# Gated mix of attention and a 2-D Fourier filter: 83 entries of a stored instruction order moved

## The chip, the cores and the metric

The kernel runs on one core of a Trainium2 chip. The core has five engines with an instruction stream each: TensorE (PE in the profile; its weight loads are PEld), VectorE (DVE), ScalarE (ACT), GpSimd (POOL) and SyncE (SP, which here only issues DMAs). ACT and POOL issue DMAs too. The metric is the device time of one execution in microseconds (us): before, the median of three runs is 454.48 us (454.02 to 456.01).

## The reference, cut to what matters

```
g = sigmoid((x * gate_w).sum(-1, keepdims=True))        # x: 2048 tokens x 640
a = attention(x @ wqkv) @ wo                            # 32 heads of 20, 8 keys: t, t-2, ..., t-14
b = irfft2(rfft2(x, axes=(-2, -1)) * (w_r + 1j * w_i))  # over tokens and features
return g * a + (1 - g) * b
```

All is float32.

## The kernel before, in words

The 2048 tokens lie on 128 partitions as 16 columns j. Everything stays on one core, and everything is written first as a recording: each engine call of the program becomes an entry of a list (`Plan.record`), 3656 in all. Then `Plan.order` reads the constant `ORDER`, a packed row of 3656 numbers. Number k says at which place of the list of what is left the k-th entry is taken out, so that this row alone fixes in which order every engine gets its instructions. `Plan.issue` emits them in that order. Each engine runs its own instructions in the order given; only semaphores, which the tile framework derives from the data and from the reuse of buffers, tie one engine to another. All instructions therefore carry one line in the profile, L385, the line that replays a recorded call, and are told apart by the names of their tiles.

The stages, by the recorded program:

- `warm`: six matmuls on zeros before the first data are there. `load_first`, `qkv_first`, `qkv`: the projection x @ wqkv, each float32 operand split in two parts of fewer bits, three products per pair. `fold`: the inputs x are loaded again (`fx0` to `fx7`, on SP's queue) and added and subtracted in mirrored pairs by DVE and POOL, for the transform along features; the raw weights `raw` come over the same queue, and ACT and POOL make the two parts `w` of them. `cols`: the transform along tokens on TensorE, copied by ACT to `zg`.
- `attend`: the sliding attention, on DVE (products `pr`, sums `L`, `s`, `o`), POOL (`pv`, scaling) and ACT (exponentials). It runs from the first third to the end beside all other stages.
- `freq(g)`, the filter groups g = 1, 2, 3, 0, 4, ..., 15, staged so that four are under way. ACT copies a slice of `zg` to `zc`; TensorE makes `v` and `u`; ACT copies `v` to `vs`; DVE forms the sum and difference `ab`; TensorE makes `x` and `z`; ACT copies `x` to `P` and, multiplied by a sign, `x` and `z` to `X`; two DMAs, issued by ACT, bring the two halves of `X` to the other half of the partitions of `P`. When both have landed, POOL multiplies `P` by the filter `wp` and adds; DVE multiplies `z` by the filter, subtracts `P`, and makes `s` of the sum and difference; TensorE transforms back in five matmuls in two pieces, `g_0` (three) and `g_3` (two), and ACT copies each piece back to `zg`. `P` and `wp` have two buffers each. The PSUM banks are one for each of `v`, `u`, `x`, two for `z`, and one for `g`, so that `g_3` of a group waits for the copy of `g_0`, and `g_0` of the next group for the copy of `g_3`.
- `load_wo`, `project_even`: the output weights `wo` are cast by ACT to their upper part and POOL subtracts to get the lower; attention rows `ot` are transposed on TensorE (`oTp`), cast by ACT to `oT` (upper part), DVE subtracts for the lower; then 15 matmuls each for `woa` and `wob`, scaled by ACT to `ya`. These lie between the filter groups.
- `spatial` (`oa`, `ob`, `ha`, `hb`) and `project_odd`: the inverse transform along features and the other half of the output projection. They close the kernel.

What a number behind a name means in the rows of an order: `P9_727` is the tile P of group 9; `oT4` belongs to token column 4.

Of the kernel before, what the change touches and what calls it, by code (L numbers as in the profile page):

```python
# [201 lines left out]


ORDER = """
T>t<81poj4|NsC0{{R31`zHT%QmDPnN2o4pqG()raQ#vzl-5Q;_f%qBd^O|&eY9QYNBMzhpDJzgbo`p?)i=NlGkg4pi)v=r_Ivh`ry`@DAn{UL<7u-|?Aw}>x~K3VSb)B{-t!WAHm))%
unAhPz4I@-2Iqv#r6L>*Xc$=jvaqQRa3b^|A+Y|WKIEEj)A@6T&9m8<23aOsCR{jD@6j{sYkO?P$b#=n<341!34nZ(X=zG8UQ{qx&71|KC<t@Gco9Z^27=SGu?TP9^_xx9CA@>m7>f!s
OYWHey&#0g11et`Jku?peeD*XENp#NW~XmY)%EME)U$cKF-Z+vV9cFqn%}p&i5#r2B6?^!L$|KiDwS5{;Iff+MQp5qs5Z*^S1D?*FMGw`(SU6f9U%OiawS(-I{rACR8a0gV^g7l@8l@~
HzRC&nZHU65UcUOIO2OqBvnhaDtej1FV1NTEP#T^)e}_RXD9Ad$LgUK7O`DNW0Ah#+vteaZ7c}l&kv=txQ?dKiO=nUU)rA`8g}=!rq`Zp$UL}3=^*VzL;nRihjg*C<t}3f%b%>5e(rGT
7-9+d=Oy~il~(PiH+y=E9&IDY*4qH(EzJ@9f5sB<6JsOb8wgocoqVcb9ZqwjK27E(DzK)a!$n^bod6w(!li>{GgdFyCb^9iu%ubjZcf$uR^!DIu<=bFg$M~+%M&!@`CRf64gryh?xA;L
=GNZz41miwBNJRJ$_PkjO#GJm*8$7Wigq;fww-$@)=FqJsud(o66Kud*z2J1AyupW9GFt;JT~7#Xc;~qw*2h&<S<LPTrE0Tvv;yIwrz$dgfpLZm!26FS+ez!;5Pt$ymK)}uVU7^YB(23  # L210
abfI)oPtr{Wh!}VC7Toq2amz>-c68x1BbhR&{(ROO)>dDpl%@SkBwsg>XhKMqNltvxU8}VnLD-Mepq&s&h0shElS}Kp$)vXuTq>iX>Cb3wH*5XM0KNCE>o-pp4<I`M~`Jd4t7#L9b*fF
wuGdJat(T)z>igeMB8%*RWQ2i06@>6iiY1>U5b|2v0EKBb^l^DfU!qWovI!Z)z_$mF)>18`>*Fx>5l*lLUh^2W>YVO>m}WBw^64&l77+nuC39&CM|*NV;F&Kj^Ppbsxdr{UH3QiDdtoE
>9^Z^(}BqP7lK<BR!aE$l*Cn@sqW=Rrb62!JRq@AUQ**c44zhaQ@t%%#OaD#xOULbqH7cNBRcpC$<;6ezVESAzEV6VDilz>dquhr&==?Ggiw{Z9m#%FDOMWi=7=f>RgP8@SK-o)kAgWc
@(~x_1gJz+dYwk6|3WH!Q+8xdEtnm+stHe=6)34-WpZL}4ugdfpv6H=3ArGy{O4l+-$ydmOvz{guh;2O#|DKW?>s2?n#?x#3TACjF=U2+g*kOcry4r$vD>c_(rzX7C1gGLLs}3NQZAtv
ogzd_!bABa9T?T3Gs=$zHA+BgpwKT1x1UyIm=uw*eDoI2ukgn(P$?v&8zZ+rqRW+=JglNr!n`th?ETZV$#&=i{iwkUtIaB@Q}*NHX-6O2z+m$sMuH>Wz2^1n{cpGSFz=vH&jcSfoL*PT
l(e3=1WK!@5fXav8#wz>T7U{iN<IAmx<(?^C_>kP7N|hYIekD3RBcpw0FDjy^s|gj!DtD#|Fe=A_=*%<#m8R@<Wb!hJG2mfgFIL-rE+7}MD)%GRQf34Eqq=3$hY_fP({XdfJ|XhJkGh*
;rddl98_KAxC_7a!PrDj$BdC~u?on-Sr!%7x<Xb-%|fGLYD;nbsQhFH`ZV2!AwjD5oZh`s>-nQReDf92g(!@sE)9XSby_X}JZC};N5m{&=tv2y?|{U!Xo}XY=9BhrsO)i~RVAUM^Zq|O
U<q^R{Fq9K0g(^bS~-#Ar7l~w9U*|gOjae1XA9=)^;WNww^WC#4NH>zmLFJ{KLbF2L~M-}VOHY45$&O!e^N2K+6x=vhq?zH#-*SPa7QY%j-TtZnWJ-SP%t-ngyr>5zN0GFY5WDlJ6xVY
J{?Q+DnkgL|4!{Sm<~W1m{#H-i#v+$kXc^Td=7heyIz#Z=u004G<&&-oRvQN>@ufMHq^=_nd~Lslju>7E|fryCi!(_@>ZcR_(2!-ffb6vQBf?!jJJpypg#Pl(ICI9d_*^JoFXsY5wOvi
nr1gFTCsh?1Z_h$3nMfvh8Bme$@%=-h{q?O6}Gk2hmQOegP}ygA~^2Iy=xmWVhfbR01Yc(!EMjd<%9@Vb+3e~4Tp1v+AlQ*{#c5SAYU<n*kAABp<2#cQRW!xhkP$v4+Q_B@o1RR^qZ=!  # L220
KeYQb+1wyz!xaZ;$|p~0Rkw(@l$#UaI{9@wGRt=OVop%vdH&C)f#pnq8#sp}eaD-%4T)cljwr&kWt(1u-yr$^T9|Th^!}&q#YLBhX4!=WaHOIid?(#4<cxl{;tI|VZp<8Df0tkOj5Jg<
zrLM3bspM%T&FVXAT;ePvu{w0-b6_nx;Ueyvynjx&1|1+Tr@Ma=vsZ;Z%(dMHq!G`SSXA%hUbZ0h8CW*EQ16manzQK<G&iL$@&h?N+WhK;95=}$gl<@C*;vSR+Gf_uMhDwcnrx&(<w#E
4@wDP2Sfe^s<4LS9>wv^@!P~EXoURBZ3aW7O{<DH;@bA%XV!^Nl&1lOHC+tpbjZ+jlWz(<xS8p*U7aet(m%YtU&)nda#i2(JfPWkJVFa(3Ltu6dk!#zpbcN{))aMKqsS^Al8l>OF@O~e
x(u+`_%sPsRi0Dl>z$t3^_s&-5k^L24nD#imbvd3lI5somyD;SGYh5p&x~Eea*h2|SPh0<Eb)zkO*`v;lUxAdI~a{fLZN`^G~L~t=1sbS`R;PB!Rn>VoOf64#iStA<yF-d%C;StyT|aY
?D(Tvdj)-E5H7x(%n1xC9d_foxjYSU#`BetY+t-WLnF^a<<=FUKyU@t&wUZ+iyz%aL&8WAup}SL^6`w!wyvn?Wk95WtV9^<2QqBYqe*mJR6-|}h$TGSv<76T!0?!B3R*cOCQAQQsOxdd
m3p$Nr6FlsqZm6&X5wW3>VG@o8cE)9LE34q+962yQajx~L(yyIq<`x{dWPvVOR`<6m}Oj6rZ{<H#`=rZh;|nIj|%8ORTVkOwbj3lhBGbTy@{(rh)-RVDCFQCvIW<2(5~_J)mPX>q56=+
Lhb>Ury!q;u}317-G@VQbSrO2)@wK#*2ey?$}g#2?U)pHv2s)pO?NC$NEZW}_=Pt^aCWSUnecEhx+Ibb?goExm{@-C0R=icvA>d;Lu2H0!_EaXeEKyk9iDqL+QBxor42ZIwFnnqAn6U3
_*)I?j(1Tb0Wru}z21ORZ9XANGt|a9GXRlDTv}|*ARx}4_pIOCIo}-%!+7EO46gQUoEI60HjiILM*_ON0>z=h9(a6jQ;n(if?QQ-d^(IxQa#o>X6Jj%Q~CVQ#tLzt$>!Z+m~oDjH=b%d
EKH_NEnnRB9(XVoDJ*@Zl675mh^pl-iALQ<c#u_7Xo3rfzTZrwxLLtlJ3eToG_xzP!s~I?WSCvyaR;y760%i;da_`9s~x8jv}!Cc#!nD;$8oY;%>}(Xu+}@7MrUZ2xihJzmNgd4?UuqQ
lj=2;{2MzSWldas;&S-TwvkI_^2-P(=+cY8NZ&KM#is{cx5Azh%rCCt_psh>;~#?CtG3B{ge&v5h$2|y{1|MIAK}+Ozghda1$mEgjpr7gMG`_IAOyi2domcj>9vTFM{B)wg*vp8$43or  # L230
Z@f{5Aex(=<zM8D2QRnY(Y^KUX#@f4ZMpYmdi0Miez?%sJ5zGB^D45Fhf?kY{c@1$1BZ*>*+bO7a5u<wOeml`7Zq-=5UqRs_6{m%aRem&IUXR;KBV&N!gweQb9B4c1dkV?z||S$8Y3m`
GISu@RzcTi>)y3qbD1XFKrjX8vHIl7reyxUS`UQ^$iw2TW_U_EB}KkdFu=o|xj{SS9^$%*xDiw}`^K^#mLU;ock7`j`Qj(AEx_NJ_6u4orvtlP9ztAo9qI(|9tWj!A}E0dnKUdKnFwf7
zGmMtKJ1JmDDk~OP7f@*?4vAi$S~Y7QPj-j!`A{ShO;R91xRW^h3#^2+-prcKnN-wL2y2hR88R2htAU;VrO5f#&*@5Bx#>?5C4ph2%gxeNLs<$8e4ZgeQr~$iv#P~$&<JH_MQ%5B)~mR
{qzhlVEVEvM0r60xftwa->^J+OYgZKQ8Ieli{hlUl(tt=31MC3VNY@y-W>Mj&!KTpf7+g&#28y108c2U0qHc4VnD^$I;|}w$0CN*1p_Gc8rT2bkG2*
"""


# [729 lines left out]
```

## Time and profile before

| | before |
|---|---|
| median of three runs | 454.48 us (454.02 to 456.01) |
| profiled execution | 455.9 us, of which the span is 453.8 us |
| TensorE busy | 440.5 us, 97% of the span |
| VectorE busy | 410.4 us, 90% |
| GpSimd busy | 364.4 us, 80% |
| ScalarE busy | 212.4 us, 47% |
| DMA moved | 110.75 MB, 244 GB/s on the mean |

Busy time is the time in which an engine's instructions ran; matmuls overlap, so a busy TensorE is one without a gap and not one at its peak. A row of the timeline gives the start, the length, the engine, and the operation as output tile <- input tiles (buffer numbers left out), with the count of instructions that it joins; a bracket at its end says how long the engine stood idle before it and which operation ended that. One float32 matmul of the program can leave two records. ACTq and SPq are DMA issues of these engines.

### The profile page before, as it was taken

To read this page: it belongs to the slowest core of one execution; us is meant where nothing else is said; L and a number is where in the kernel's file an instruction comes from. 1 tells how busy PE (TensorE), PEld (TensorE's weight loads), DVE (VectorE), ACT (ScalarE), POOL (GpSimd) and SP (SyncE) were. 2 spreads that over 40 slices of the span, in tenths; PEclk is the share of its full clock that TensorE was granted. 3 is DMA by queue.
4 is the path that set the end of the run, shared out by engine and by line. 5 is a ranking of instruction groups with operands and counts; after the bars stand their busy time and mean duration, and the time that the engine had idled before them with its cause. 6 is when DMAs were issued, how large, how long until landed. Compare 5 with 4: busy or idle time off the path is not lost. (4 is left out here: it accounts for less than half of the span.)

```text
span 453.8 us, 7246 instructions
## 1 busy us (share of the span) xinstructions
PE 440.5 (97%) x2440; PEld 390.1 (86%) x2440; DVE 410.4 (90%) x519; ACT 212.4 (47%) x561; POOL 364.4 (80%) x316
## 2 busy tenths in 40 slices
PE   8999999999999999999998999999989999999996
PEld 6888888888888888899886789989877899999996
DVE  4999999799999999999989999989899997899484
ACT  4724254444236454255457665666554554342110
POOL 1158895599999999997987998976999988879720
PEclk9999999999999999999999999999999999999999
DMA  8998999688868989679969888979884231364832
GB/s 317 389 370 285 380 300 379 244 252 284 230 192 259 364 243 315 171 243 315 311 207 290 258 269 262 287 222 315 264 241 105 82 97 59 127 193 137 282 133 87
DMA packets 73956, 110.75 MB, mean 244 GB/s; under 512 B 21296, under 2 KB 50992, under 8 KB 73920
## 3 DMA queue, kind: packets, MB, share of 16 engines
q1 hardware_dynamic: 40192, 69.32, 46.8%
q10 hardware_dynamic: 32816, 36.97, 26.3%
q0 software_dynamic: 912, 4.00, 2.2%
q8 instruction: 19, 0.31, 0.3%
q14 instruction: 17, 0.14, 0.1%
HBM read 72.51 MB, written 32.84 MB: 232 GB/s over the span
## 5 line engine op out<-in xcount | busy, mean ns | idle before, releaser
L385 PE MATMUL qkv<-w,xo 128*128 128x480 f32 (+1 forms) x480 | 110.9, 386 | 0.3 <-ACT zg L385 0.3
L385 PE MATMUL qkv<-w,xe 128*128 128x480 f32 (+1 forms) x474 | 104.3, 381 | 0.0
L385 PEld LDWEIGHTS qkv<-w,xo 128*128 128x128 f32 x480 | 89.8, 189 | 14.3 <-ACT zg L385 0.7
L385 PEld LDWEIGHTS qkv<-w,xe 128*128 128x128 f32 x474 | 89.2, 188 | 14.8 <-ACT xe L385 0.6
L385 ACT COPY ev<-qkv 128x480 f32<-128x480 f32 x64 | 34.8, 556 | 39.7 <-PE qkv L385 31.8
L385 PE MATMUL woa<-wo,oT 128*128 128x320 f32 x240 | 47.2, 318 | 0.5 <-ACT oT L385 0.3
L385 PE MATMUL wob<-wo,oT 128*128 128x320 f32 x240 | 46.9, 315 | 0.2 <-ACT ya L385 0.2
L385 POOL TENSOR_TENSOR P<-P,wp 128x963 f32<-128x963 f32 (+1 forms) x16 | 35.3, 2209 | 6.8 <-DMA P<-X 4.7
L385 PEld LDWEIGHTS woa<-wo,oT 128*128 128x128 f32 x240 | 37.7, 188 | 1.4 <-ACT oT L385 0.6
L385 PEld LDWEIGHTS wob<-wo,oT 128*128 128x128 f32 x240 | 37.8, 188 | 0.6 <-ACT ya L385 0.4
L385 POOL TENSOR_TENSOR fx<-fx 128x160 f32<-128x160 f32 (+1 forms) x16 | 12.8, 817 | 24.0 <-DMA fc<-in_t_fc 16.9
L385 POOL TENSOR_TENSOR w<-raw,w 128x480 fp32r<-128x480 f32 (+1 forms) x20 | 24.8, 1263 | 5.1 <-ACT w L385 5.0
L385 ACT CAST oT<-oTp 128x384 fp32r<-128x384 f32 (+1 forms) x32 | 13.4, 428 | 31.4 <-PE oTp L385 14.6
L385 PEld LDWEIGHTS g<-mm,s 128*128 128x128 f32 x150 | 21.1, 190 | 8.0 <-ACT zg L385 5.6
L385 PE MATMUL g<-mm,s 128*128 128x128 f32 x150 | 23.9, 281 | 3.6 <-ACT zg L385 3.4
L385 DVE TENSOR_TENSOR oT<-oTp,oT 128x384 fp32r<-128x384 f32 (+1 forms) x32 | 15.3, 487 | 10.5 <-ACT oT L385 10.4
L385 PE MATMUL oa<-gt,zg 128*128 128x161 f32 (+1 forms) x96 | 24.0, 344 | 0.0
L385 PE MATMUL ob<-gt,zg 128*128 128x161 f32 (+1 forms) x96 | 22.1, 344 | 0.0
L385 PE MATMUL v<-bt,zc 128*128 128x240 f32 (+2 forms) x96 | 21.1, 325 | 0.4 <-ACT vs L385 0.3
L385 ACT CAST w<-raw 128x480 fp32r<-128x480 f32 (+1 forms) x30 | 17.3, 594 | 8.1 <-PE qkv L385 3.6
L385 PE MATMUL u<-bt,zc 128*128 128x240 f32 (+2 forms) x96 | 20.1, 322 | 0.7 <-DVE ab L385 0.7
L385 DVE TENSOR_TENSOR fx<-fx 128x642 f32<-128x642 f32 (+2 forms) x24 | 19.2, 800 | 0.7
(304 smaller groups left out, 1106.3 us busy)
## 6 DMA issues: line engine op xcount, KB each, us to landing
qkvd<-ev ACTq DMA_DIRECT2D x32, 480.0 KB, 5.2
wp<-in_ws SPq DMA_DIRECT2D x16, 642.0 KB, 5.1
raw<-in_wqkv SPq DMA_DIRECT2D x25, 240.0 KB, 6.9
fx<-in_x SPq DMA_DIRECT2D x8, 641.0 KB, 8.2
ot<-od SPq DMA_DIRECT2D x16, 320.0 KB, 4.0
P<-X ACTq DMA_DIRECT2D x30, 160.5 KB, 4.4
fd<-fx POOLq DMA_DIRECT2D x6, 640.0 KB, 7.0
f<-fd SPq DMA_DIRECT2D x6, 640.0 KB, 6.5
```

The source lines that it names most:

```text
L385: p.dve.memset(w, 0.0)
```

## The change

Only the constant `ORDER` differs. Each engine gets the same instructions as before; 83 of the 3656 entries stand some places earlier or later. Of the text of the constant two lines stand for all, since its characters tell a reader nothing:

```
 ORDER = """
-T>t<81poj4|NsC0{{R31`zHT%QmDPnN2o4pqG()raQ#vzl-5Q;_f%qBd^O|&eY9QYNBMzhpDJzgbo`p?)i=NlGkg4pi)v=r_Ivh`ry`@DAn{UL<7u-|?Aw}>x~K3VSb)B{-t!WAHm))%
...
```

What it does to the engines' own orders is seen at three places below; a minus is a row of before, a plus a row of after, and a row with neither is in both. The other moves are these. At the start the sixth warm-up matmul stands with the five others and no longer between the first projection matmuls. On SP's queue the loads of `fx4` and `fx5` stand behind four of the five loads `raw2_0`, `raw2_2`, `raw2_1`, `raw2_3`, where they stood ahead of all five. Some casts, folds and attention steps change places with a neighbour in the projection stages. In the filter groups a half of `ab2` on VectorE and the reduction `s7b` go ahead of one attention reduction of `L6a`; `pr5a` goes ahead of `ab7`; on TensorE `x13` goes between the matmuls of `g10_0` and ahead of a transposition; on ACT the second `P` DMA of groups 2, 12, 14 and 15 is parted from the first by copies, as in the first place below. Late in the kernel some matmuls of `woa` and `wob` change places.

ACT, filter group 9, beside the transposition for token column 4:

```order
 L385 ACTIVATE X9_730<-z9_729,sign_325 128x321
 L385 ACTIVATE X9_730<-x9_728,sign_325 128x321
-L385 DMA P9_727<-X9_730 64x642 x2
+L385 DMA P9_727<-X9_730 64x642
 L385 COPY zg_211<-g6_3_712 128x32x8
 L385 CAST oT4_831<-oTp0_832 128x384
 L385 COPY vs11_748<-v11_747 128x321
 L385 COPY P9_727<-x9_728 128x321
+L385 DMA P9_727<-X9_730 64x642
 L385 COPY zg_211<-g7_0_724 128x48x8
```

The second of the two DMAs that exchange the halves of group 9 stood right behind the first and now stands behind four ACT instructions: the copy of `g6_3` to `zg`, the cast of `oT4`, and the copies `vs11` and `P9`.

POOL, between the filter multiplications of groups 2 and 3 (`pv7b` is an attention product, `wo6` the lower part of an output weight):

```order
 L385 TENSOR_TENSOR P2_618<-P2_618 128x321
-L385 TENSOR_TENSOR wo6_334<-wor4_339,wo5_333 128x320
+L385 TENSOR_TENSOR pv7b0_495<-vt7b_485,L7b_487 128x8x80
 L385 TENSOR_TENSOR L6a_503<-L6a_503,m6a_508 128x256
-L385 TENSOR_TENSOR pv7b0_495<-vt7b_485,L7b_487 128x8x80 x2
+L385 TENSOR_TENSOR pv7b0_495<-vt7b_485,L7b_487 128x8x80
 L385 TENSOR_TENSOR wo6_334<-wor4_339,wo5_333 128x320
 L385 TENSOR_TENSOR P3_631<-P3_631,wp3_622 128x963
```

Of the two subtractions for output weights that stood ahead of the multiplication of `P3`, one is gone from there; it stands behind the addition of `P4`, two filter groups later.

TensorE, filter group 15 and the projection of token column 8:

```order
 L385 MATMUL v15_800<-bt_326,zc15_799 128x161
 L385 MATMUL u15_802<-bt_326,zc15_799 128x240
+L385 MATMUL g11_0_778<-mm10_731,s11_766 128x128 x3
+L385 MATMUL woa8_849<-wo0_328,oT8_845 128x320
 L385 MATMUL u15_802<-bt_326,zc15_799 128x161
-L385 MATMUL g11_0_778<-mm10_731,s11_766 128x128 x3
-L385 MATMUL woa8_849<-wo0_328,oT8_845 128x320 x3
+L385 MATMUL woa8_849<-wo0_328,oT8_845 128x320 x2
 L385 MATMUL woa8_849<-wo1_329,oT8_845 128x320
```

The three matmuls of `g11_0` and one of `woa8` now stand ahead of one `u15` matmul that stood ahead of them.

## Rows read from the trace of the kernel before

**Rows 1.** Stretches: us, busy us of each engine (instructions), granted clock, DMA share, GB/s.

```profile
10.00:100.00 90.00, 90.00 (x414) 77.67 (x413) 81.97 (x94) 39.53 (x96) 61.05 (x64) 1.00 0.92 324
230.00:350.00 120.00, 112.62 (x680) 98.61 (x679) 112.17 (x168) 74.46 (x211) 104.71 (x83) 1.00 0.83 255
350.00:400.00 50.00, 50.00 (x316) 45.97 (x315) 43.94 (x56) 25.17 (x67) 44.90 (x37) 1.00 0.34 98
```

**Rows 2.** TensorE's waits: us in total, times, longest us.

```profile
PE g L385 <- ACT zg L385: 3.4, 7, 0.9
```

**Rows 3.** Timeline of ACT at group 9: start, us, operation, idle before.

```profile
294.93 1.12 ACTq L385 DMA_DIRECT2D P<-X  x2
296.09 0.37 ACT L385 COPY zg<-g 128x256 f32<-128x256 f32 x1 [1.23 <-PE u L385]
296.36 0.48 ACT L385 CAST oT<-oTp 128x384 fp32r<-128x384 f32 x1
297.04 0.46 ACT L385 COPY P<-x 128x321 f32<-128x321 f32 x1
```

**Rows 4.** Timeline of TensorE at that place (`g` is `g7_0`).

```profile
296.51 0.94 PE L385 MATMUL g<-mm,s 128*128 128x128 f32 x6 [0.59 <-ACT zg L385]
```

**Rows 5.** Timeline of VectorE there (the lower part of `oT4`).

```profile
296.87 0.56 DVE L385 TENSOR_TENSOR oT<-oTp,oT 128x384 fp32r<-128x384 f32 x1 [1.04 <-ACT oT L385]
```

**Rows 6.** Timeline of POOL there (the multiplication of `P9`).

```profile
302.13 2.27 POOL L385 TENSOR_TENSOR P<-P,wp 128x963 f32<-128x963 f32 x1
```

**Rows 7.** Timeline of ACT at group 1.

```profile
237.22 0.47 ACTq L385 DMA_DIRECT2D P<-X  x1
237.48 0.44 ACT L385 COPY P<-x 128x321 f32<-128x321 f32 x1
```

**Rows 8.** Timeline of POOL ahead of the multiplication of `P3`.

```profile
256.92 0.88 POOL L385 TENSOR_TENSOR wo<-wor,wo 128x320 fp32r<-128x320 f32 x1
257.75 2.23 POOL L385 TENSOR_TENSOR P<-P,wp 128x963 f32<-128x963 f32 x1
```

**Rows 9.** The tile P from 250 to 262 us: durations in ns, first and last start.

```profile
L385 ACTq DMA_DIRECT2D P<-X x2: 507/545/583, 250.2 to 250.8; - x2
...
DMA to landing us min/median/max: 4.5/5.4/6.4
```

**Rows 10.** Timeline of VectorE at groups 2, 3 and 0.

```profile
241.35 0.48 DVE L385 TENSOR_TENSOR ab<-u,vs 128x321 f32<-128x321 f32 x1
...
244.37 0.89 DVE L385 TENSOR_TENSOR ab<-u,vs 128x321 f32<-128x321 f32 x2
...
260.02 0.50 DVE L385 TENSOR_TENSOR z<-z,P 128x321 f32<-128x321 f32 x1 [0.69 <-POOL P L385]
```

**Rows 11.** Timeline of TensorE at groups 2, 11 and 13.

```profile
241.99 0.78 PE L385 MATMUL z<-ab,mm 128*128 128x321 f32 x2 [1.01 <-ACT X L385]
...
323.47 0.84 PE L385 MATMUL u<-bt,zc 128*128 128x240 f32 x4
324.51 0.94 PE L385 MATMUL g<-mm,s 128*128 128x128 f32 x6 [0.20 <-ACT zg L385]
...
336.32 0.94 PE L385 MATMUL g<-mm,s 128*128 128x128 f32 x6 [0.93 <-ACT zg L385]
```

**Rows 12.** Timeline of POOL: the multiplications of `P11` and `P14`.

```profile
314.62 2.27 POOL L385 TENSOR_TENSOR P<-P,wp 128x963 f32<-128x963 f32 x1 [2.50 <-DMA P<-X]
...
335.57 2.24 POOL L385 TENSOR_TENSOR P<-P,wp 128x963 f32<-128x963 f32 x1 [0.67 <-DVE oT L385]
```

**Rows 13.** The tile P from 312 to 325 us, its DMA issues.

```profile
L385 ACTq DMA_DIRECT2D P<-X x4: 468/538/1414, 316.6 to 323.2; - x4
```

**Rows 14.** Timeline of SP in the fold stage.

```profile
21.71 6.39 SPq L385 DMA_DIRECT2D raw<-in_wqkv  x5
```

**Rows 15.** The tile fx from 14 to 46 us: issue to landing of its DMAs.

```profile
DMA to landing us min/median/max: 5.0/8.2/11.8
```

**Rows 16.** Timeline of VectorE: the first fold step of `fx4`.

```profile
36.89 1.11 DVE L385 TENSOR_TENSOR fe<-fx 128x642 f32<-128x642 f32 x1 [0.85 <-POOL fx L385]
```

More of the change, by code (lines that the diff above doesn't have):

```diff
@@ L204 @@
 ORDER = """
[L205 to L232, printed above, removed]
@@ L233 @@
-zGmMtKJ1JmDDk~OP7f@*?4vAi$S~Y7QPj-j!`A{ShO;R91xRW^h3#^2+-prcKnN-wL2y2hR88R2htAU;VrO5f#&*@5Bx#>?5C4ph2%gxeNLs<$8e4ZgeQr~$iv#P~$&<JH_MQ%5B)~mR
-{qzhlVEVEvM0r60xftwa->^J+OYgZKQ8Ieli{hlUl(tt=31MC3VNY@y-W>Mj&!KTpf7+g&#28y108c2U0qHc4VnD^$I;|}w$0CN*1p_Gc8rT2bkG2*
+T>t<81poj4|NsC0{{R31`zHT%QmDPk&^9H>y=H*?`Lk%9Gnl%)B_CdQV7rLsIrccwJ*XZFz*xqYeRBjZrov+5#L1Oh`|S-vka{>Ev@`BNPpDi;@qu&*-YHs`Aj<=o4M|U7=fMhWee;NX
+^76~28J1S@!p3vwI-9h+#|Ck?nchch@CwN@6<&cfS)KONwNQ$Ga4yW1Wg;KFNlgT%!}iZ7AZ@S9#C`?KZO90~YLNpD$dnc;XF9Z$v<)8e`TBAsr;AL*h=*JvGLc*|Jgc;N7E)DBr}aA?
@@ new lines @@
+f;sWbp0sDen0**VL5%&Munzyqy}w>Mct^Pvu0~l5-`D_u0Id<ss_5>P<e;EYGm1VbKRBN@2Yax646Kg6hm_Y^{@V5GLffFrC3yqWS-1Dq*OBXez4DaG>!T#D*Y|}!<{41@<HkCgAN0wo
+3pLz@1^%q`Qa1(2$(t>!fg@sI@fq4RCdfCAs*g088vJt)1x~)=p>pNE(wUnttuXhP$S@%llCK8&{D{VtP1_=Lc-T^W(&{}TQp}zi{wndmm)1D!*_zPbdf0EGGc|%gxx%!#EIk50J;6>!
+&BLtLs5mfaIIo1-_XC`c-;lYag#++FnHSSM<q`EYKeoS;EB2(zNm>cG9eR-xwBXL3({qRr)aRe%i87V(Cx<}t!m$Rb?z^SoE$(P4hvp9%4_e$hxxM27;1%VqS&?$MK235+@}{5-9ln-q
+;|NcrPW?Ajq+z0_{=Ld}KP(I$PnOZNdSs4iJIM*PD_V_Uf*qGA#s8EQSAeGW=OM^k+txbLNOe0TdEJ5CG#H!IS@ga3BkZ$$g(Kwd@{eu0IS2U6Fl%}8=8}XQffJpqf`q&Li`t!S71O+`
@@ new lines @@
+T3K;aCzfJo_UkGi<I~=_#eC4-S+|$zURJZxIp1DS(+5Kjp4|%rWX!tPFpOZX7x2{Q@i%iWfb&n`y3V=y&RPB3BDGSb6Dn0}Qq*nQaB_hc6_~qPr%!Dq;a13`fIO<n2Ol&!=-Xw`l7OX<
+yswVb_x)Lo7NIDYQ3W8*rmTbei*74>fsi$7y+O0?#m`x+Gic>d@1`974wSR881hT-hcR$aPrS0Vzo08j5}o!HNS%-rfKjWq_dA(v$Nh6W5aI5m%t|Esn^e6N)RD(dA)&b#@*ow_C0|Pd
+xyQSigF&v*p*;64z@Fv&9)n3sapOu-P^~{5jdNN`Mjjd-UVLVcz-neT?EAfW+xReB{8C`x2|G!}7#KQ3&~Seyz0ITw-ft|N1CWWm-?d?hOhB5c63Od`_-;%<Nr?(FSpm;_+b9{xE)?Ee
+pYes1Ycz+;#c@PJZ+xousx&`&%xb2PgCJ;$u#IV9NrKz~nQRDxbNH+U^^3x8GjCyQ$Ra_+bK{UN@_2<n42u_jq8svw9&r)7naSj~5ZsHEXpa2rnI$lSiDg`u9<tgtdhqQAV5BOXtphJv
@@ new lines @@
+h%KJf7_YiO#RGD*dC2dwUn&(>46k>!;%`^c7Q7U{Xp!<VW~t_|0B4>zqo{cPS+dumkKu5+2RFWDUmT3s&e8gvF0Y|_j%<GOs2Ta8OYK7thh|*6XI@fe2jvvnJfe*&N|s5Wjt2)hUeg96
+svSZ9g>Q4zlATt3zt}D?NP0l-kF!STbZbT+u1>r<k*|lbp=7&pjzK-q1+45A|HqU&YGR#=58+eX4h3#w$N2p&bh_h51I*SM)ls&N_z)QiBo<r7Ar8ALZhNiB<NMb~*Z%3@e9-hJcIy#p
+)A_Zrh*`X){Cu4!IxddSvLER=UYoc=WHhfoe$dfOjKhX~l;@uVOb0t4N$gFm=>3c$Z?^=xI+!peT@SI{W)&9ms_2p$(jp)Zg^Z~9wl@%reMyO>rh4q<rIthr|AdAXIqSy042(IJfg_Ty
+Fa#k~KDW%r`X_H7lnD25yVm?r(R=D-Mmb9@r&IO(VwGY32ko;p{YI`P9BIL4N(2p*f?J;|YY5*XK$X*?x?dakia{Um1Pf@uZSPJPz|tVFd*EkJ2VV8c;v>I=mGF`j*VZ$;{0$5t-RhJW
@@ new lines @@
+0z-&!%~dt{=rhZ>8UM`ka4B}}Z`vm40u&K|!cZe+=K9eoHl+)jNA%>QQH}clli+)-LoeJ&`_{b7y*nBq{AmVJ&0lXh{sYE0ze+;K)FXPLKsRK3p1Wzu=?mgtx3=x<^_dj8A(>YI!gpiO
+5QUoECE}twC~+s+nzHjH6||-7Z&ZULas|n}%Q;FkFh}X<jscuDsf_3M^*Q6NEvqBlgVVSsOt{iL?n%4Le~b~#9Px=V%2s*q(W2^}-Hszvy@J<tQK{Q)z@_P=g7uDa7AuGQ<31U3kio(W
+^6q^Vf`mXg6jScc=2tXK@x*i{msx0G*d%<|E`;M&@e3*cZl_Obi^JL80*EGeT>D_Hc<7ZFQ2}H`ImvkDjTKZ}H{xqSice*PPggKTzKR@EJE10SAA3xZgV=R)K&i>fr`cEZZ2n;9T!LDO
+u4*3YLyT_At=#BKIp%Y7rBzN}9~&xca>zwP>yF^R40mC4UrEhHtwKqYS_jxicc4o5-8P^7B%+32JHt`wK0eS5U4(SKp|m<^6ggYqek>Gq8=f`!UYzgz!B0(3Y`1DWYdWH{cqj)tq7W68
@@ new lines @@
+svT!$pIlDPH$>YhX#s7G<Tlv%l;CVgD-tPP!fA@DXEL+R@$z{C-U(=4u_TCr(;S+qG4mB<-HH9r7)Pi}jbHk-3<)kloP2Cr!V1e4L|nhKHTiwNzod?kHZNr?Fq}elW`ExNmz)*16-|3*
+lCEE8OT2}OuvZrZAQW2LFZis1``j>EM5{S)YLS=)YO2D=!dF(U0H1JiLq_BZdpdYeq|7#uu#>l}`>0(n<vqr<m+Al7rHe}uiG>>M^}NJ_#OKi+5)({gWSep*m|(i9fwcv_w}2~f9pEWw
+ZR<dqnRb=v39lMhBDk+AFMS$yeo2^IJi0Cmu9nQAs*Rfri9o5!=tfu2fk80+CKI=U`2{XNHU?235jn6BhtTRjS<-5Yy2a$m^!;Q6Di^~@{SvFS>%5EdBM#AyUi+D~SGrgdZ61QZeF(Qd
+wvZHz*+-Dj-7#JTKu=&YsEPsHo$}W5uuYXch*wJNtpH8y9WBohPzsBLJEb;R4N`JG$4Jc%<BS!LsE>W0h1LOu7BKK*c-w`D-%8m#b8XyfV2=Azw+V>~6mvWbD=9|y3aZk23_wS8wc8Ki
+)Bmlo^(cDZt|V1yyClSWKWfjNXFv&gu|hz1z9$M;;3%bSn9D)HGK@$EMr!7<lBW<ruGvz)HB6!Ntg0bVPxUe6^={SbZZqVG&d(ju_+a4B4z(Ng&ZDKGO_GVChL-!H*RV_GB|H*VDnGk}
@@ new lines @@
+qk?pcgy4<I*o@g&cK%Vxy@hca&u-G3l;X<ZEdm%4L;ZIG_Qa)3b|^c4kGhgY9Q9`p>C?*tBrq_gt1FMlf;zMqg!+72coFN*X;o2en`6MJGq&=sG^Kq2RzRy3NsKnP|25_r<vB&upy%b3
+Tq(@S`~B>hl(O^REBq9|HS7J*SSD2pcQxTYfNIO$di2)ScYF)#qfX&@{>3fJKt%3F?7`(meG`W%Er9wnnxr<u++Dn$Ud;rhg0u{oPSEUCGu&lCligRvw?o8eOlzGmDhLB*@@FRX#eQf|
+|4FngJ+4Fy-nys1(Cz@jJdn-zm&ELLykpEGPRr%4Fk&n>7E1hCZ4`F+$Yq%r+mBen-Q?%@WHC+Qw#rw?N>>Sm;oSc{oGp9ZB(;STgdlv;p@l34e7i<DMxVf5jQvD)2!=D=;0O0vzo?YQ
+KU~OAamN2gKnZp&`R-AU1mV!cX{>+)=1N6_5LfHd*x#Ht74Zy37)PgCM;whE#$jyJ1ns(m{S#5)p4_QM5Y=dUb+qOohkne-z`hAQb)@pN@FuyQ@Rg?-{OYAfUuB<D>0FWeE?OM~tMt=5
@@ L235 @@
+8rhh?RZJtS=r}drfp<4noR#V-m}IaU!clT04XdC$EYQ<11A_<lUISjI9-`sve<gNFN~sH(1|T!$esq@fB_VTaGYVuqY^KtoDZaQ*Ykw=gxd)x-|KZaczO5j$Hmtt}oJP{>GbBl0jSHnf
+X6jUso^ecD>|lQ2g$sD@1S5OE-C&szc%G5P7*dFT3{vLk;#@Z*BEM;9_$%l#vtkPo#eojJKugxw5mZUzfVv<3e0V{9Cm!x(tSgsV-JjSnmbbw>FvxB3E-eEj%U}gPD6{S1<5IM%__Rul
+Q~ack^Q^dbG?dNv-=KqloV8h4Wr2W=rk2sG<USKmHPR)BIE0(*vAZKtfF_a=0DuzHllPjuLk!T&J4lM>lY?iIrv6zPHVJ(B{x6`GMP+0lOAaZ1<jw#8od1Df
 """
```

## The prediction

> **What bounds the kernel now.** I read the stretches first. In each, the reader is to see whether TensorE's busy time equals the stretch's length. From 10 to 100 us and from 350 to 400 us it does, to the last hundredth; from 230 to 350 us, where the filter groups lie, it is 112.62 of 120, so 7.38 us are open there [rows 1]. The granted clock is 1.00 in all of them, so no move can win or lose clock. A stage in which TensorE has no gap gives nothing for a reordering of the same matmuls: the kernel's end is the end of the filter groups plus work whose length is fixed. So only the filter stretch is worked out below, plus one place in the projection stage that could open a gap. VectorE is as full there as TensorE, 112.17 of 120, and POOL has 104.71: three engines wait for each other in turn, and what one of them gains is easily met by the next. TensorE's waits come second: the largest sum, 3.4 us in 7, is that of the back transforms `g`, for ACT's copies to `zg` that free their bank [rows 2].
>
> **The change part by part.** All durations are from the profiled execution, 455.9 us long (span 453.8, so 2.1 lie outside). It lies inside the spread of the three runs, 1.4 above their median. I work out a difference and set it against the median, 454.48.
>
> Warm-up, folds, attention and projection moves before 230 us: no instruction is added, TensorE stays without a gap, so 0. VectorE or POOL may gain a step earlier, but the attention takes its operands at the pace of TensorE's output, and the filter groups can't begin before the projection's last matmuls. One exception, the loads of `fx4` and `fx5`, is the rival at the end. The moves after 350 us are 0 for the same reason: full TensorE before, and the same matmuls in another order.
>
> Group 9. Before, ACT issued both exchange DMAs in a row, 1.12 us for two, and the copy of `g6_3` began only at 296.09, after 1.23 us idle; the cast of `oT4` followed at 296.36 [rows 3]. TensorE's `g7_0` waited 0.59 for that copy [rows 4], and VectorE 1.04 for that cast [rows 5]. The second issue goes behind four instructions. So copy and cast come one issue earlier, 1.12 / 2 = 0.56. TensorE's wait shrinks by 0.56 of 0.59, VectorE's by 0.56 of 1.04, and both are engines without other slack here: -0.56. It can't be more than 0.59. At worst it is +0.15: the second half arrives later by the time ACT takes over four instructions, and POOL, which began `P9`'s multiplication at 302.13 straight from its last product [rows 6], waits for it. What the later place costs is read from group 1, where before already had copies ahead of the second issue: there the DMA was issued at 237.22, before the copy to `P` that stands ahead of it had begun, at 237.48 [rows 7]. The issue runs ahead of the engine's work, so I take no delay that POOL sees.
>
> [...]
>
> POOL ahead of `P3`. One `wo6` subtraction, 0.88 us, leaves its place; `P3`'s multiplication began right behind it at 257.75 [rows 8]. It can move forward by at most 0.88, but no further than its halves' landing: the second DMA was issued at 250.8 and the longest DMA of the two took 6.4 us, so 257.2 or a little later [rows 9]. What it gains is 257.75 - 257.2 = 0.5; I take 0.45. VectorE stood 0.69 idle for this result at 260.02 [rows 10], so the gain reaches it whole, and TensorE through it: -0.45, bounds -0.69 and 0. The subtraction comes back behind `P4`'s addition, where it pushes an attention product and `P5`; the weight `wo6` is not read before the first `woa`, several us later. If that cover fails, it costs 0.88 once.
>
> `z2` and `x3`. TensorE waited 1.01 before `z2`; the row puts it down to ACT, but what came last was the second half of `ab2` on VectorE at 241.35 [rows 10, 11]. That half goes ahead of a reduction, so `z2` starts about a microsecond earlier. But VectorE has the same work to do before `ab3` at 244.37, and `x3`, the next to need it, waits in place of `z2`: -0.05, bounds -0.4 and +0.25.
>
> `g11_0` ahead of one `u15` matmul. `g11_0` waited 0.20 at 324.51 for ACT's copy, behind two `u15` matmuls that took 0.84 [rows 11]. One of the two, by its columns (161 of 401) a third, 0.3 of that, no longer covers the wait. The copy does not come earlier for it. So the wait grows by 0.27 and the matmul is done after it: +0.27, bounds 0 and +0.35.
>
> Groups 14 and 15: as in group 9, a copy goes between two DMAs. TensorE's 0.93 before `g13_0` at 336.32 [rows 11] shrinks by about 0.6, but what ends this stretch is `s15`, through POOL: `P14`'s multiplication at 335.57 stood idle 0.67 before it; the row names VectorE's `oT`, which has no part in `P14`, so I take the landing of its halves for the cause [rows 12], and `P15`'s multiplication follows in line. I put 0; bounds -0.6 and +0.4 (the copy delays the second half of `P14`). Other moves in the stretch (`x13` into `g10_0`, `pr5a` ahead of `ab7`, the store of `o7b`) put an instruction ahead of a wait of the same length or into a place with more than a microsecond to spare: 0, bounds -0.1 and +0.2.
>
> Sum: -0.56 - 0.45 - 0.05 + 0.27 = -0.79. The bounds added up the way independent pieces spread give about -1.7 to +0.8. The prediction is 454.48 - 0.79 = 453.7; by the profiled execution's own time it would be 455.9 - 0.79 = 455.1. The likeliest case's own range is 452.8 to 455.3.
>
> **The rivals.**
>
> *Nothing comes through.* The exchange DMAs set POOL's steps: it stood 2.50 us idle until `P11` had landed, and `P14`'s wait ended most likely by one too [rows 12]. If these landings stay where they are, -0.56 and -0.45, both earlier, are waited away. For it: DMA share 0.83 in the stretch [rows 1], so a transfer issued earlier need not land as much earlier. Against it: the issue hangs on `x` and `z`, which follow TensorE's place. Time: 454.5.
>
> *More comes through.* TensorE's 7.38 us of gaps are many short waits, nearly half of them for one kind of copy on ACT [rows 1, 2], and five of the moves put copies or casts ahead of DMA issues. If each round of the groups gets a little shorter, a third or more of the 7.38 goes: 454.48 - 2.8 = 451.7. For it: waits in rounds add up. Against it: VectorE's own 7.83 us of gaps is all that it can give, and its work is unchanged.
>
> *Exchange halves come later (slower, little).* Place: ACT at groups 12 and 14. Group 12's second issue took 1.41 us where 0.54 is the median [rows 13], so it was held already; now two copies stand ahead of it. With the copies of rows 3 as price, 0.37 + 0.48 = 0.85 for group 12, and 0.37 for group 14, each reaching the end through POOL: +1.2, and the gains above halved, -0.3: 454.48 + 0.9 = 455.4. It decides from the point at which the second issue waits for the copies to be executed and not only passed on.
>
> *The fold's loads come too late (slower).* `fx4` went out ahead of the five `raw` loads, which took SP 6.39 us to issue, until 28.10 [rows 14]. Now `fx4` goes out behind four of them, at about 27 to 28. Its landing takes 5.0 to 11.8 us [rows 15], so 32 to 39.9; VectorE wants it at 36.89 [rows 16]. At the median, 8.2, it is there by 36.3; at the worst 3.0 us late, then VectorE's and POOL's folds, and after them POOL's weight parts for the next projection, shift by it and open a gap in the full stretch: 454.48 + 3.0 - 0.4 = 457.1 with half of the gain. It decides from a landing later than 36.9 plus what POOL has to spare.
>
> That the change doesn't do what it says is no rival: the rows of the order show the moves.
>
> **How the numbers follow.** Chances: forecast 0.41; nothing comes through 0.15; more 0.23; halves later 0.12; loads late 0.09. About 0.5%, 2.27 us, is what a measurement of this kernel can tell from no change, so the bounds are 452.2 and 456.75. Faster: of "more" 0.18 lies below 452.2, of the forecast 0.02: 0.20. Slower: of "loads late" 0.08, of "halves later" 0.04: 0.12. The rest, 0.68, is the same. The range for 8 in 10 is 451.4 to 456.6: below it lie 0.08 of "more", above it 0.08 of "loads late" and 0.03 of "halves later".
>
> **What would show each step.** Right, if the copy of `g6_3` starts about 0.6 us behind the first issue for `P9` instead of 1.16, `g7_0` waits under 0.1 and the cast's VectorE wait is near 0.5; if the wait of VectorE for `P3` falls below 0.3; if TensorE has a gap of 0.4 to 0.5 before `g11_0`; and if TensorE's busy time from 230 to 350 us is about 0.8 higher. Wrong, if that busy time is unchanged although the single waits went (the first rival), if it rises by 2 or more (the second), if POOL's idle time ahead of `P12` and `P14` grows (the third), or if TensorE shows a gap between 60 and 75 us and VectorE a wait for a DMA near 37 us (the fourth).

## The result, and the profile after

The changed kernel takes 457.09 us (median of 16 runs, 455.41 to 459.35), the kernel before in the same sessions 455.69 (16 runs): a ratio of 1.004, interval 1.0025 to 1.0054. So it is slower by 0.4%, about 1.8 us; the medians differ by 1.4. Forecast were 453.7 and a range up to 456.6. Of the 3.4 us between forecast and median, 1.2 are the base: the forecast was set against three runs of the kernel before (454.48), and 16 runs give 455.69. The profiled execution of the changed kernel took 458.67 us, span 456.9.

First the stretches of the profile after, which answer to [rows 1]:

```profile
10.00:100.00 90.00, 88.70 (x406) 75.93 (x405) 78.17 (x95) 38.86 (x96) 57.83 (x63) 1.00 0.92 321
150.00:230.00 80.00, 78.66 (x418) 69.36 (x417) 78.12 (x70) 36.81 (x99) 73.05 (x59) 1.00 0.86 273
230.00:350.00 120.00, 112.87 (x679) 98.95 (x678) 112.03 (x169) 74.12 (x210) 103.68 (x81) 1.00 0.88 261
350.00:400.00 50.00, 50.00 (x313) 45.61 (x312) 44.20 (x51) 24.33 (x65) 45.58 (x39) 1.00 0.29 82
```

The reader is to see that the filter stretch, on which the prediction was worked out, hardly changed (112.87 of 120 busy, 112.62 before), and that TensorE now stands idle where it was full: 1.30 us between 10 and 100 and 1.34 between 150 and 230. From 20 to 225 us TensorE is busy 204.68 before and 201.73 after: 0.32 us of gaps became 3.27. From 225 to 352 us, the filter groups in every kernel here, gaps of 7.38 became 7.13. These two sums are used as "projection gaps" and "filter gaps" below. One gap stands near 142 us in both kernels, and its growth is not the change's doing: p9_only, described below, has the order of before up to 294 us and no gap there. TensorE's timeline, before and after:

```profile
141.90 10.28 PE L385 MATMUL qkv<-w,xo 128*128 128x480 f32 x46 [0.32 <-ACT zg L385]
143.80 8.57 PE L385 MATMUL qkv<-w,xo 128*128 128x480 f32 x38 [0.64 <-ACT zg L385]
```

TensorE's waits after, largest first (us in total, times, longest):

```profile
PE g L385 <- ACT zg L385: 2.7, 6, 0.6
PE qkv L385 <- ACT zg L385: 2.0, 2, 1.3
PE v L385 <- ACT vs L385: 1.2, 2, 0.8
...
PE qkv L385 <- POOL w L385: 0.9, 1, 0.9
...
PE qkv L385 <- ACT w L385: 0.4, 1, 0.4
```

The wait for the `g` copies fell from 3.4 to 2.7 [rows 2]; three waits of the projection `qkv` are new or larger, and the experiments below show that most of the loss is in them.

**First gap, 62 to 67 us.** ACT's timeline in the fold stage, before:

```profile
33.36 0.56 ACT L385 COPY ev<-qkv 128x480 f32<-128x480 f32 x1 [3.43 <-DMA qkvd<-ev]
...
36.52 1.02 ACT L385 COPY ev<-qkv 128x480 f32<-128x480 f32 x2 [1.46 <-DMA qkvd<-ev]
...
40.70 1.09 ACT L385 CAST w<-raw 128x480 fp32r<-128x480 f32 x2 [0.44 <-DVE fx L385]
```

and after:

```profile
39.59 1.02 ACT L385 COPY ev<-qkv 128x480 f32<-128x480 f32 x2 [7.09 <-DMA qkvd<-ev]
...
45.86 0.56 ACT L385 COPY ev<-qkv 128x480 f32<-128x480 f32 x1 [3.59 <-DMA qkvd<-ev]
...
46.32 0.60 ACT L385 CAST w<-raw 128x480 fp32r<-128x480 f32 x1
```

POOL's (the first row is of before), and below it TensorE's:

```profile
59.78 5.97 POOL L385 TENSOR_TENSOR w<-raw,w 128x480 fp32r<-128x480 f32 x5
...
46.99 2.41 POOL L385 TENSOR_TENSOR w<-raw,w 128x480 fp32r<-128x480 f32 x2 [4.27 <-ACT w L385]
...
62.45 5.96 POOL L385 TENSOR_TENSOR w<-raw,w 128x480 fp32r<-128x480 f32 x5
```

```profile
66.10 10.08 PE L385 MATMUL qkv<-w,xe 128*128 128x480 f32 x45 [0.94 <-POOL w L385]
```

Read from the end: TensorE waits 0.94 for a weight's lower part, from a block of five on POOL that began at 59.78 before and at 62.45 now. POOL is late because it stood 4.27 us at 46.99 for ACT's casts of `w2`, with fold steps queued behind. ACT cast at 46.32 (40.70 before) because a copy of the projection's output, `ev1_2`, now stands ahead of the casts, and it waits for an output buffer whose store had not landed. And the stores land late. Two of them, issued by ACT at 33.42 and 34.49 before, landed after 3.1 and 3.6 us; after, the same two go out at 29.64 and 30.75 and land after 9.9 and 10.4 (KB each, us from issue to landing):

```profile
qkvd<-ev ACTq DMA_DIRECT2D x1, 480.0 KB, 3.1
qkvd<-ev ACTq DMA_DIRECT2D x1, 480.0 KB, 3.6
...
qkvd<-ev ACTq DMA_DIRECT2D x1, 480.0 KB, 9.9
qkvd<-ev ACTq DMA_DIRECT2D x1, 480.0 KB, 10.4
```

ACT's 3.43 at 33.36 before was for the store ahead of these two, which took 12.8 us then and 8.9 after. So the slow landing passed from one store to the next two, and the pair of copies that started at 36.52 starts at 39.59.

**Second gap, 206.75 us.** ACT's and TensorE's timelines before:

```profile
200.25 0.32 ACT L385 COPY qbank<-q7b 128x160 f32<-128x160 f32 x1
200.65 0.59 ACT L385 COPY zg<-z 128x512 f32<-128x512 f32 x1
...
203.27 3.54 PE L385 MATMUL qkv<-w,xo 128*128 128x482 f32 x15
```

ACT's, VectorE's and TensorE's after:

```profile
204.57 0.30 ACT L385 COPY qbank<-q7b 128x160 f32<-128x160 f32 x1 [1.44 <-DVE pr7a L385]
204.80 0.58 ACT L385 COPY zg<-z 128x512 f32<-128x512 f32 x1
```

```profile
203.05 1.49 DVE L385 TENSOR_TENSOR pr7a<-kt7a,qbank 128x1280 f32<-128x1280 f32 x1
204.90 1.49 DVE L385 TENSOR_TENSOR pr7a<-kt7a,qbank 128x1280 f32<-128x1280 f32 x1 [0.36 <-ACT qbank L385]
```

```profile
206.75 3.56 PE L385 MATMUL qkv<-w,xo 128*128 128x482 f32 x15 [1.34 <-ACT zg L385]
```

ACT's copy of a third of `q7b` into the tile `qbank` (128 x 512 float32 in PSUM, by the kernel's text) starts 0.03 us after the product `pr7a6` has ended, though that product reads another third of the tile; behind the copy stands the `zg` copy whose bank TensorE needs. And the next product, `pr7a4`, waits in turn for that copy, though its own third was filled long before.

### The profile page after: what moved, and what is told of

The parts are those of the page before. It is cut to its first block, busy times and chain, and to the rows that moved or that the text cites. A ratio compares the mean times of both kernels' runs of the same rounds, so it can differ in the third digit from the quotient of the medians.

```text
span 456.9 us, 7241 instructions
## 1 busy us (share of the span) xinstructions
PE 441.0 (97%) x2440; PEld 389.9 (85%) x2440; DVE 407.2 (89%) x519; ACT 211.1 (46%) x561; POOL 361.8 (79%) x316
## 5 line engine op out<-in xcount | busy, mean ns | idle before, releaser
L385 PEld LDWEIGHTS v<-bt,zc 128*128 128x128 f32 x96 | 16.0, 189 | 4.0 <-ACT vs L385 1.9
```

What stands on the lines that cost most here:

```text
L385: p.dve.memset(w, 0.0)
```

## The experiments

Four theories stood against each other: the displaced loads (A) or the moved copy (B) make the first gap; a tie over the whole `qbank` tile (C) or lateness as such (D) makes the second. Each kernel below was run 12 times, beside 35 runs of the kernel before. The gaps are the stretch less TensorE's busy time in one profile each, and the second column is the time of the execution that was profiled.

| kernel | ratio to before (95%) | profiled, us | projection gaps, us | filter gaps, us |
|---|---|---|---|---|
| before | 1 | 455.9 | 0.32 | 7.38 |
| changed | 1.004 (1.0025 to 1.0054) | 458.67 | 3.27 | 7.13 |
| loads_back | 0.9988 (0.9973 to 1.0003) | 453.35 | 1.38 | 5.57 |
| ev_back | 1.0019 (0.9999 to 1.0039) | 457.43 | 1.40 | 8.31 |
| pr_after_copy | 1.0004 (0.9989 to 1.0019) | 454.97 | 1.32 | 6.40 |
| filters_only | 0.9973 (0.9955 to 0.9992) | 453.68 | 0.55 | 6.41 |
| both_mended | 0.9967 (0.9948 to 0.9987) | 453.57 | 0.00 | 6.50 |
| loads_and_ev | 1.0043 (1.0023 to 1.0064) | 456.3 | 0.93 | 7.00 |
| pr_only | 1.0033 (1.0015 to 1.0052) | 457.88 | 1.42 | 8.43 |
| p9_only | 1.0000 (0.9982 to 1.0019) | 455.83 | 0.00 | 7.89 |

The profiled time less both gap sums is 446.4 to 448.4 us in all ten rows, so the gaps carry most of the differences. But the runs of one kernel spread over 2.5 to 4.6 us, and the filter gaps differ with the execution: they are 7.00, 7.38 and 8.43 in three kernels whose filter groups have the same order (loads_and_ev, before, pr_only). A difference of 1 us in the last column shows nothing by itself.

**loads_back.** Against the changed kernel, in which `fx4` stands behind four of the raw loads and `fx5` behind all five, on SP:

```
 DMA fx3_129<-in_x
+DMA fx4_131<-in_x
+DMA fx5_133<-in_x
 DMA fx6_135<-in_x
...
 DMA raw2_3_157<-in_wqkv
-DMA fx4_131<-in_x
 DMA raw2_4_159<-in_wqkv
-DMA fx5_133<-in_x
```

> The changed kernel with one undoing: on SP's queue the loads of fx4 and fx5 stand again ahead of the raw loads, as before the change. Theory A (the two loads, now issued at 28.9 and 29.9 us beside ACT's qkv stores at 29.6 and 30.8, make these stores land late, so ACT idles 7.1 us at 39.59 and TensorE's 0.35 + 0.94 us gaps at 62 to 67 us follow): both gaps vanish, ACT's wait at that place falls to about 3 us, time 457.1 - 1.3 = 455.8. Theory B (ACT's copy of ev1_2, now ahead of the casts of w2, holds these casts until a store has landed at 45.86): the gaps stay at 0.8 us or more, time 456.8 to 457.1. In both, TensorE's 1.34 us gap near 207 us stays.

The gaps at 62 to 67 us are gone. ACT's timeline of this kernel:

```profile
36.19 1.02 ACT L385 COPY ev<-qkv 128x480 f32<-128x480 f32 x2 [1.60 <-DMA qkvd<-ev]
...
42.09 0.56 ACT L385 COPY ev<-qkv 128x480 f32<-128x480 f32 x1 [2.05 <-PE qkv L385]
...
42.55 0.59 ACT L385 CAST w<-raw 128x480 fp32r<-128x480 f32 x1
```

The two stores of above land after 3.2 and 3.7 us, so the moved copy waits only for TensorE, and the casts come 3.8 us earlier than in the changed kernel. The loads are needed for the gap. The 1.38 that is left is the second gap.

**ev_back.** Against the changed kernel, on ACT:

```
-COPY ev1_2_143<-qkv1_2_142
 CAST w2_0_152<-raw2_0_151
 CAST w2_1_154<-raw2_1_153
 DMA q0a_342<-qkvd
 CAST w2_2_156<-raw2_2_155
+COPY ev1_2_143<-qkv1_2_142
```

> The changed kernel with one undoing: on ACT the copy of ev1_2 stands again behind the three casts of w2_0, w2_1, w2_2, as before the change. Theory A (late stores by the displaced loads): the casts still come about 2 us later than before the change, POOL's and VectorE's folds and POOL's weight parts with them, and a gap of TensorE of 0.3 to 0.8 us stays at 62 to 67 us; time 456.3 to 456.8. Theory B (the copy ahead of the casts): the gaps there vanish; 455.8. The 1.34 us gap near 207 us stays in both.

Here, too, the gaps at 62 to 67 us are gone, though the stores stay late:

```profile
39.53 1.02 ACT L385 COPY ev<-qkv 128x480 f32<-128x480 f32 x2 [6.97 <-DMA qkvd<-ev]
...
42.64 1.09 ACT L385 CAST w<-raw 128x480 fp32r<-128x480 f32 x2 [0.44 <-DVE fe L385]
```

The casts no longer stand behind a copy that waits for a store. So neither A nor B alone: the late stores and the copy ahead of the casts are needed together. The time alone does not show this: 1.0019 has an interval that overlaps with the changed kernel's. Its filter gaps, 8.31, belong to one of its longer executions (457.43; the median of its runs is 455.48, 1.6 below that of the changed kernel).

**loads_and_ev.** The kernel before with the moves of the two edits above made, and `raw2_2` earlier on SP (as plus and minus above, the other way round).

> The kernel before with three moves alone: fx4 and fx5 behind the raw loads, raw2_2 earlier on SP, and ACT's copy of ev1_2 ahead of the casts of w2. Undoing either the loads or the copy took the gaps at 62 to 67 us away, so the theory is that it takes both together. Then the pair alone makes TensorE gaps of 0.8 to 1.3 us at 62 to 67 us, and the time is 1.002 to 1.003 of before. If another of the moves in the folds (on VectorE or ACT) is needed too, there is no gap, or one under 0.3 us, and the time is that of before.

```profile
65.87 1.34 PE L385 MATMUL qkv<-w,xe 128*128 128x480 f32 x5 [0.81 <-POOL w L385]
```

The gap is back, in the kernel before, by these moves alone; no other move in the folds is needed. The time, 1.0043, is as long as that of the whole change. The runs of this kernel spread from 455.29 to 459.92, those of p9_only from 454.15 to 456.64; its one profile (456.3 us) is among the shorter, so the gap is likely larger in others. That was not seen in a profile.

**pr_after_copy.** No engine's order differs from the changed kernel. In the common list alone one entry stands elsewhere (entries of other engines between these are left out):

```
-DVE pr7a6_475<-kt7a_468,qbank_63
 ACT zg_211<-z4_0_299
 ACT qbank_63<-q7b_486
+DVE pr7a6_475<-kt7a_468,qbank_63
```

> The changed kernel with every engine's own order unchanged; only in the common order in which the instructions are handed out does VectorE's pr7a6 come behind ACT's first copy of q7b to the qbank tile and no longer ahead of it. Theory C (the framework ties reads and writes of the whole qbank tile, though the copy and the product touch different thirds of it; so the copy waited for pr7a6 until 204.54 us, ACT's zg copy behind it waited too, and TensorE 1.34 us at 206.75): the copy waits for pr7a2 alone, the zg copy follows at about 202.5 us, TensorE's gap near 207 us is under 0.2; time 457.1 - 1.3 = 455.8. Rival D (the zg copy is late because VectorE and ACT are late as a whole by the gap at 62 to 67 us): nothing changes, the gap stays at 1.2 to 1.4 us, 457.1. The gaps at 62 to 67 us stay in both.

The second gap is gone. ACT's timeline of this kernel:

```profile
202.18 0.30 ACT L385 COPY qbank<-q7b 128x160 f32<-128x160 f32 x1
202.41 0.59 ACT L385 COPY zg<-z 128x512 f32<-128x512 f32 x1
```

The copy waits for nothing, and now `pr7a6` waits 0.32 us for it. VectorE's timeline:

```profile
202.52 2.88 DVE L385 TENSOR_TENSOR pr7a<-kt7a,qbank 128x1280 f32<-128x1280 f32 x2 [0.32 <-ACT qbank L385]
```

Theory C holds: which of the two waits, the copy 1.44 us for the product or the product 0.32 us for the copy, was fixed by the place in the common list, where the framework ties the whole `qbank` tile. Rival D falls: the gap at 62 to 67 us is still there (0.79).

**pr_only.** The kernel before with VectorE's three moves at that place:

```
 DVE L7a<-pr7a2_473
+DVE pr7a6_475<-kt7a_468,qbank_63
 DVE pr7a4_474<-kt7a_468,qbank_63
 DVE s3b_461<-L3b_455
+DVE L7a<-pr7a4_474
 DVE o3a4_449<-pv3a6_451
-DVE L7a<-pr7a4_474
 DVE s3b_461<-s3b_461
-DVE pr7a6_475<-kt7a_468,qbank_63
+DVE pr7b0_488<-kt7b_484,qbank_63
 DVE L7a<-pr7a6_475
-DVE pr7b0_488<-kt7b_484,qbank_63
```

> The kernel before with VectorE's three moves alone: pr7a6 ahead of pr7a4, the sum of pr7a4 ahead of o3a4, pr7b0 ahead of the sum of pr7a6. Whole-tile theory: ACT's first copy of q7b waits for pr7a6, the zg copy behind it with it, and TensorE has a gap of 1.0 to 1.4 us at 203 to 204 us; the time is between that of before and 1.003 of it, as the filter groups find VectorE and ACT further on. If the gap of the changed kernel came from its lateness by then, there is none.

```profile
204.40 2.90 PE L385 MATMUL qkv<-w,xo 128*128 128x482 f32 x12 [1.42 <-ACT zg L385]
```

The gap is there without any lateness, 1.42 us, and the time is 1.0033 of before.

**filters_only.** The kernel before with the moves from about 225 us on, none earlier (52 of the 83 entries).

> The kernel before with only the moves from the last projection matmuls on (from about 225 us): filter groups and tail as in the changed kernel, warm-up, folds and projection as before. Prediction's sum (filter moves give 0.8 us): TensorE's gaps from 225 to 352 us fall from 7.3 to about 6.5, time 0.998 of before, 454.9. Rival E (the filter stretch gives back what each move gains, since the profile of the changed kernel has 7.1 us of gaps there): gaps 7.0 to 7.4, time as before within 0.3 us. Rival F (the moves cost in themselves, and the loss of the changed kernel sits here): gaps 8 or more, 456.5 or more.

The prediction's sum fits here: 0.9973, or -1.2 us (-2.0 to -0.4) for -0.79. The one profile has filter gaps of 6.41, about 1.0 less than that of before. The places that the prediction spoke of, TensorE's timeline of this kernel:

```profile
241.50 0.78 PE L385 MATMUL x<-ab,mm 128*128 128x321 f32 x2 [1.43 <-DVE ab L385]
242.12 0.71 PE L385 MATMUL z<-ab,mm 128*128 128x321 f32 x2
...
247.72 1.22 PE L385 MATMUL v<-bt,zc 128*128 128x240 f32 x6 [0.76 <-ACT vs L385]
...
260.62 0.70 PE L385 MATMUL z<-ab,mm 128*128 128x321 f32 x2
...
295.42 0.83 PE L385 MATMUL g<-mm,s 128*128 128x128 f32 x6
...
322.76 0.94 PE L385 MATMUL g<-mm,s 128*128 128x128 f32 x6 [0.48 <-ACT zg L385]
```

**p9_only.** The kernel before with one move, that of the first order fence above (`P9`'s second DMA on ACT).

> The kernel before with one move alone: the second exchange DMA of group 9 behind the zg copy of g6_3, the cast of oT4, vs11 and P9 on ACT. The prediction's term: the zg copy starts about 0.6 us behind the first issue and no longer 1.16, TensorE's wait of 0.59 before g7_0 falls under 0.1, VectorE's 1.04 before the lower part of oT4 to about 0.5, POOL's multiplication of P9 is not later, gaps from 225 to 352 us 7.3 - 0.6 = 6.7, time 0.9988 of before. Rival: a wait further on takes its place; gaps there 7.2 or more, time as before.

At its own place it does what was forecast. ACT's timeline:

```profile
294.45 0.47 ACTq L385 DMA_DIRECT2D P<-X  x1
294.96 0.37 ACT L385 COPY zg<-g 128x256 f32<-128x256 f32 x1 [0.58 <-PE oTp L385]
295.06 0.51 ACTq L385 DMA_DIRECT2D P<-X  x1
295.23 0.48 ACT L385 CAST oT<-oTp 128x384 fp32r<-128x384 f32 x1
...
320.95 2.08 ACTq L385 DMA_DIRECT2D P<-X  x2
```

The `zg` copy starts 0.51 us behind the first issue (1.16 before), and TensorE's `g7_0` at 295.39 has no wait. The time is that of before, 1.0000, but its interval is 0.8 us wide to either side, so the forecast of 0.9988 is not excluded by it. In the profile the filter gaps did not shrink (7.89). What is late next stands in the last row: the two issues for group 13 take 2.08 us (1.12 for two in [rows 3]), and the copy behind them, which frees `g10_3`'s bank, comes late, so that `g11_0` waits 1.17 (0.20 in [rows 11]). It still starts 0.74 earlier than before. That is lost at POOL's `P14`, which starts 0.95 later than in [rows 12]: the second half, issued at 329.3, took 7.0 us to land, where it took 5.3 before. TensorE's and POOL's timelines:

```profile
323.77 0.94 PE L385 MATMUL g<-mm,s 128*128 128x128 f32 x6 [1.17 <-ACT zg L385]
...
345.04 0.91 PE L385 MATMUL g<-mm,s 128*128 128x128 f32 x6 [1.22 <-DVE s L385]
```

```profile
336.52 2.27 POOL L385 TENSOR_TENSOR P<-P,wp 128x963 f32<-128x963 f32 x1 [2.29 <-DVE oT L385]
```

So this profile shows what the rival says, waits further on that take the place of the one that went; the times can't tell the rival from the forecast. What made the second issue for group 13 long (1.57 us) is open. In the built program it waits only for the load of `mm13`, which had gone out at 310.85 and landed 4.8 us later. SP's issue of the store of `o6a`, at 322.11, took 0.91 us instead of 0.37 and ended at the same moment. Such an issue is not new: one for group 12 took 1.41 before [rows 13].

**both_mended.** The changed kernel with the edits of loads_back and pr_after_copy together.

> The changed kernel with two undoings together: the loads of fx4 and fx5 ahead of the raw loads as before the change, and pr7a6 handed out behind ACT's first copy of q7b. If the two gaps (62 to 67 us, and near 207 us) are the whole loss and the filter moves keep their gain, TensorE has under 0.6 us of gaps from 20 to 225 us and 5.5 to 6.5 from 225 to 352 us, and the time is 0.995 to 0.998 of before, 453 to 454.3. If the filter stretch gives the gain back when it is reached earlier, its gaps are 7 or more and the time is that of before.

Projection gaps 0.00, filter gaps 6.50, 453.89 us, 0.9967 of before. It is faster than both kernels by its interval against before, and as fast as filters_only within theirs.

## Why the prediction was wrong

**The step that failed** is the first of the change's parts: "no instruction is added, TensorE stays without a gap, so 0" for the moves before 230 us. A full TensorE was taken as proof that these moves could not matter. At most it says that TensorE has no gap there for them to close. Two groups of moves opened 2.63 us of gaps there (0.35, 0.94 and 1.34), and in the profile after, TensorE reached the filter groups 2.6 us later. By the times, loads_and_ev is worth +2.0 us, pr_only +1.5 and filters_only -1.2: 2.3 in sum for the 1.8 of the whole change, which is within their intervals. One exception was weighed, the two loads; `ev1_2` ahead of the casts and `pr7a6` ahead of `pr7a4` were not.

**The rival "the fold's loads come too late"** (0.09) named the right move, the sign, and POOL's weight parts as the way to TensorE, with the wrong mechanism. That its time, 457.1, is the median that was measured is luck: it is made of a late `fx4` (+3.0) that did not come, and of a base that was 1.2 too low. It priced the landing of `fx4` itself against 36.89 [rows 16]. After, the slowest `fx` landed in 8.8 us (11.8 in [rows 15]), and VectorE began `fx4` at 37.39 after the same 0.85 us for POOL. What suffered were ACT's stores: the two loads went out at 28.9 and 29.9 us, beside stores at 29.6 and 30.8, and ACT waited until 39.59. That the place of the loads makes these stores late is shown (9.9 and 10.4 us to land, 3.2 and 3.7 in loads_back); by what mechanism is not. Even that needed the moved copy: ev_back has the late stores and no gap. I argued from who waits for the moved transfer, and not from which other transfers are under way at its new time.

**The filter terms.** The profile of filters_only is compared with that of before. The first five waits are alike in the other five kernels with the filter moves, and as before in loads_and_ev and pr_only, which have none of them:

- Group 9, -0.56: TensorE's 0.59 is gone, as put. What it is worth in time is not shown: by itself the move gave nothing that is clear of noise (p9_only). The issue went out ahead of older work, as in [rows 7]: at 295.06 in p9_only, ahead of the cast at 295.23 and the copies at 295.60 and 295.92 that stand before it. But where two issues took 2.08 us, from 320.95 to 323.03 (p9_only), the cast that stands behind them started only at 323.07.
- POOL ahead of `P3`, -0.45: VectorE's wait of 0.69 for POOL [rows 10] is gone, and `z4`, which VectorE's step lets go, starts at 260.62 without a wait (0.52 before). POOL waited 0.19 for `P3`'s DMA, so the landing was the bound, as put.
- `g11_0`, +0.27: its wait is 0.48, before 0.20 [rows 11]. Right.
- `v4`, for which the sum has no term: its wait is 0.76, before 0.31.
- Groups 14 and 15, put at 0: 0.98 us of waits at 332 to 335 us, before 1.27.
- `z2` and `x3`, -0.05: right in size, wrong in place. The two halves of `ab2` changed places, so the 1.01 before `z2` and the 0.40 before `x2` became one wait of 1.43 before `x2` (241.50 above), and `x3` did not wait.

The transposition behind which `x13` stood no longer waits its 0.36, but it doesn't in p9_only, loads_and_ev and pr_only either, where `x13` was not moved; so that is no gain of the move.

These waits add up to -0.65. So the sum of -0.79 fits, with +0.45 overlooked, and it was for the wrong part of the program. In the profile of the changed kernel itself the filter gaps are 7.13. Whether the gain is smaller there because the stretch is reached 2.6 us later, or because a longer execution was profiled (458.67, median 457.09), one profile cannot tell. Of this execution's extra 2.6 us at TensorE's end (450.2 to 452.8), the projection gaps are 2.95, less 0.35 at the start and 0.25 in the filters; the other 0.3 was not traced.

## What to carry to other kernels

Where an engine has no gap, the moves beside it have none to close, and are not harmless (here they opened 1.30 us between 10 and 100 and 1.34 between 150 and 230): for each move in such a stretch, look at what its engine waits for at the new place and who stands behind it. A transfer that is moved can change the landing of others that are under way at its new time (here from 3.1 us to 9.9), so list those, and what waits for them. Where instructions are handed out by a framework from one common list, that list can decide which of two accesses to a tile waits for the other (here 1.44 us on ACT or 0.32 on VectorE), even if each engine's own order is the same.

## What the runs showed that was not expected

- Waits went by the whole tile. A copy into one third of the `qbank` tile waited for a product that reads another third, 1.44 us; with the product behind the copy in the common list, it waited for nothing, with all five engines' orders unchanged. The tile lies in PSUM; whether tiles in SBUF are tied as wholes too, no run here shows.
- Two 641 KB loads issued beside two 480 KB stores: these took 9.9 and 10.4 us to land, and 3.2 and 3.7 with the loads put back.
- The same order of the filter groups gave TensorE gaps of 7.00 to 8.43 us from one kernel to the next, a spread wider than the 0.79 that the filter moves were forecast to gain.
